# Attention in a conformer block: engine, bank, buffer and order of every key tile from tables

## The chip, the cores and the metric

One core of one Trainium2 chip. A core has five engines that run their own instruction streams and meet through semaphores: TensorE (PE, matrix products into PSUM; PEld is its weight load), ScalarE (ACT), VectorE (DVE), GpSimd (POOL) and SyncE (SP, which here issues most transfers). The metric is the device time of one launch in microseconds; the median of three runs before the change is 894.57 us.

## What is computed

Two sequences of 4000 tokens with 144 features pass through a conformer block: a half-step feed-forward layer, attention with 4 heads of 36 features over all 4000 keys, a gated convolution of 5 taps, a second half-step feed-forward layer, and a layer norm ahead of each and at the end.

```python
B, T, D, K, H = (2, 4000, 144, 5, 4)
h = _layernorm(x)
x = x + 0.5 * (_silu(h @ w_ff1a) @ w_ff1b)
qkv = _layernorm(x) @ w_qkv
scores = jnp.einsum('bhqd,bhkd->bhqk', q, k) * Dh ** (-0.5)
p = _softmax(scores, axis=-1)
x = x + einsum('bhqk,bhkd->bhqd', p, v) (heads joined) @ w_o
a, b = halves of _layernorm(x) @ w_pw1
c = depthwise convolution of a * _sigmoid(b) with dw
x = x + _silu(c) @ w_pw2
x = x + 0.5 * (_silu(_layernorm(x) @ w_ff2a) @ w_ff2b)
return _layernorm(x)
```

## The kernel before

**Tiles.** Tokens are cut into 16 chunks of 500 (8 per sequence). A chunk's queries meet the keys of their sequence in tiles of 64 keys: 62 full tiles and one rest of 32, so 63 per chunk and 1008 in all, numbered `n` in the order of `its`. For a full tile PE makes the scores of four heads with four products of 64x64 (`scores`, two per half `hh`), each filling one quarter of the array, into two PSUM banks of 128 x 500 f32. Six of the eight banks serve scores and all other products; the last two (`BX`, `BX+1`) hold the chunk's output sums.

**Exponentials.** A tile's exponential is made in one of two ways. ACT does it with one activation over both banks (128 x 1000, `emit_exp`), and the result goes to one of 11 buffers `PT`. Or DVE does it (`dve_tile`): one conversion to int16 per half out of PSUM (z), then two bit operations (y and w) and a product (m) between `PT` buffers. The DVE way leaves two factors in two `PT` buffers, and both are multiplied with V. PE then adds a `PT` buffer times V to the output sums (`o_quads`), 4 products for a tile of ACT and 8 for one of DVE. The softmax needs no maximum; a column of ones in V gives the denominator.

**The rest.** `pre` makes the first feed-forward layer and K, Q and V of a chunk; those of the first sequence have to come ahead of its attention, and the ones of the second sequence run between key tiles. So do `post1` (output product, gate) and `post2` (convolution, second feed-forward layer, store) of finished chunks. Sigmoid and SiLU are made with tanh, which lies in one activation table with exp; the last chunks use SiLU itself, for which ACT loads another table. Layer norms take statistics on DVE, the power and the scaling on POOL (`XN`), then a DMA transpose on SP's queue. `ln_trq` copies the transposed chunk into `XTQ` with two DMAs, one for each half of the features.

**Order.** A planner (`Rec.op`, `Sched`, `pick`) simulates the engines with costs (`c_pe`, `c_dve`, `c_act`) and latencies, and so chooses which tile goes to DVE (`due`), which bank and buffer each gets, and the order on each engine. Each step of the planner is a block of instructions. `Rec.reorder` (line 249) then moves the blocks of each engine by up to 45 places with the table `ORDER`, and `PLACES` replaces the planner's choice of banks. `Rec.finish` derives the waits from the dependences, and `Rec.replay` (line 343) emits everything. It emits every instruction at one line, L353, so that the profile's lines say nothing and its groups are told apart by tile names: `PS<-QT,KT` are scores, `PT<-PS` exponentials or DVE's conversions, `PT<-PT` DVE's other operations, `PS<-PT,VA` output sums, `TH<-PS` the tanh.

```python
shift = [ALPHABET.index(c) - 45 for c in table[e]]
...
for i, blk in enumerate(blocks):
    assert at[i + shift[i]] is None
    at[i + shift[i]] = blk
lines[e] = [o for blk in at for o in blk]
```

Of the kernel before, what the change touches and what calls it, by code (L numbers as in the profile page):

```python
# [12 lines left out]
D = 144  # L13
# [20 lines left out]
ALPHABET = '!#$%&()*+,-./0123456789:;<=>?@ABCDEFGHIJKLMNOPQRSTUVWXYZ[]^_`abcdefghijklmnopqrstuvwxyz{|}~'  # L34
ORDER = {
    "pe": (
        'PPPPPPPPPPPPQQRROKPPQRPQLPPQOPPSOROQLQOQOPPPPXPNPUkNOJLPLPQOLPNOOOOPPMOOOOOOOROOPPPQOPPPPPPPTPNPNQTN'
        'PNOROOPQTUMRO]KKOYZZMK]KKKKKOKPHOPRULNPPMPQQNQQNPZOOZOOOOOINNPNPQOPPPPPPPPPPPPPQQQMPQRNQNQOQOQRNQQMQ'
        'SNVVMMWYMMMPNGSMRSSKRSSHRJMQOPPPQOPPPPPPPQOQOQOPPQOPQOPPPQRRMQRLRNOQQQMQOPQQQVLOOOOOPPPQOPPPPPRSNNQN'
        'SSNNQMRPNROOROUNOTNNSMRMRMQNPQQRMOPPQOQQQMPQOPPPQQNPPSPNOPPQOPPQQNPPPPPPPPPPQOQOPQOQOPPQQNPPPPPQOQQQ'  # L40
        'MPQOPPQOPQOPQOPPPQOQQNPPPPQOQOPPPQQQMPPQQQQQKPROQQMPPQOPPQOPQOPQRNQNPPPPPQSNOQNPPPPPPQOPPPPPPQOPPPPP'
        'PPPPPPPPPPPPPPPPPPPPPPRPQQLPPPPSOOOPPPPPPPPPPPPPPPPQOPPPPPPPPPPPPPPPPQRPMQOPQOQQNPQOQQNQOPSOOOPPPPPP'
        'PPPPPPROOQOPPPPPPQOPPQOPPPPPPPPPPPQOPPPPPPPPPPQOQOQRNQNROQNPQQRMQNPPPPPQOPPPPQOPPPPPPPPPPPPPPPPPPPPP'
        'PPPPPPPQOPPSOOOPPQOPPQOQOPPPQRNOQOPQOPQOPPQOPPROQQMQOPQOPPQQNROOPPPPPPPPQOPPQOPPPPQOQOQOPROOPQOPPPQO'
        'SOOOPPQOPPSOOOPPSOOOPPQOPPSOOQNPQOPQOPQSNOQNPSSNRMMRPNPQOPPQQQMPQOPPPQQQQLPROQNPPPPQQNQOQOPPPQQQMQOP'
        'RORNQNPPPPPQSNOQQMQSNOOPPROQQQLPQOPQOPQOPPQOPPPPPPPQOPPPPROOPPSOOOPPQOPPPPPQOPPPPQOPQOQOPPQOSPPQLPQO'
        'QOPPPTOOORNOQQQMPPPPPPPQOPPPPPPQOPPPPQOPPPPPPPPPPPPPPPPPPPPPPQQNPPPPPPPPPPQQQMPRPNQOPPQQQRLOROOQOROO'
        'PPPPPPPPPPPTOSNOMPPPRROMQOVOOOOOOPPPPPPQQNPPPSOOOPPQOPPPPPPPPPPPPPPPPPPPPPQOPPPPPPPPPPQQNQOPQQNQOPPP'
        'QOPPPQOROOPQSNOOPPSOOOPPQOPPPPPPQOPPQOPPPQOROOPSOORNOPPROOPPPQOPPPRPQRROJPPQOQOPPQQNPPPPPQOPPPQOQOPP'
        'PPPPQOPPPPPPQOPPPPPPQOPPPPPPPPPPPPPPPPPPPPPPQOPPPPPPQOPQOPPPPPPPPPPQOPPQOROOQOPPPPPPPQOPPQOPPPQOPPPP'  # L50
        'PPPQOPPPQOPPPROOPPPPPPPPPPPPPPPPPPPPQOQQNPPQOPPQOPQOPPQOPPPPPPPPQOPPPPPPPPPPPROOPPPPPPPROOPPPPPPPPPP'
        'PPPPPPSOOOPPPPPSSNNNPQOPPROOQOPPPPPPPPQOPQQQMPPPPPPPQQNPQOPPTOSNOSLORNOPPQOPPQQNPPTOPRRLRLOPPROOQOTQ'
        'NNOPPPPPPPPPPQOQOPROOPQQNPROOQOPPQOPPQOPPPPPPPPQOPPPPPQOPPQOQOQSNOOPPQQNPQOQOPPPPPPPPPPQOPPQOPPQOPPQ'
        'OTOOOOQQRMQNQOPPPQQNROOPQOPPQRVMNOOROMROOPPPQOPPPPPSOOSNOOPQOPSOOQNPPPPPPPPPPQOPPPPTOOOOPQOPPPPPPPPP'
        'PPPPQOPPPPPPPPPPQOROOPPQOPQOPPROOQOPQQNPQOPQOPPQOPSSNNNQQNPQUNOPNOPPPPQOROOPPQOPPQOPQOPSOOOPPPTOQNNP'
        'PPPQOPPPSOPQMRORRMUPPPPQHPPPPQOQOPPSOOOPUOOOOOPQOPPSOOOPPPPPPPPPPPQRROQRPQQGPTTOMOMROOPPPPPPPPQOROQN'
        'PPQOPPPQOPSOPQMPPRPNPRPNPQOPPPPPPPPPPPPPRPNPQQNPPPPPPPPPPQOPPPROQNPPQQNPPPQOPQOPPPPPPRRNNPPPQOQSNOQN'
        'PTOOOQNPPPPPPPQOPPQQQMPROOPQOPQOQOPPPPQOPPPPPPPPPPPPPPPPPPPPPQOPPPPPPPPPPPPPPPPPPPPROOPPQOQOPQOROOSO'
        'OUNOOUNPQLQMPROOPQOPROOQQQQQKPQOPPPPPPQOPPPQOPQRNRNQNQQQMRRSNLQNQOPQOPPPPPPPROOPPPPPPPPPPPQOPPPQOPQO'
        'PROOPQQNPPQQNPPPPPPPPPQOPQOPPROOROOPPQQTMOPNPPPPPPRPNPPQOPPPPPPPPPPPPPRPQSPKOQQQMPPPRORNQNPROOPRRNNR'  # L60
        'OQNPQOQQNPPPPPPROOPPQOPPQOPPPROQRMRRMNQOPQOPQQNPROOQOPPPPPPPPQOPPPPPPPPRPNPPSOOQNQOPSOOOPPPPPPPPPPPP'
        'PPPPPPPPQOQOPQRNQNPPPPPPQOPPPPPPPPPPPPPQORRNNPPPPPPPPPPPPQOPPQOPPPQQQQLPQOQOPPPPPPPPPUOQNSOLOPQOQOPP'
        'QQQMPRPNPPPPPPPQQNPPROOPQOPQOQQNPPPQOQOPPQOSOOTNOOOWQTMMNNNPQOPPPPPSOOQNSPNQSMRNRMQQMPPTOPVMPTLPRLRP'
        'JPPQOPPRPNQQNPPPPPPQOPQOPPQOPQOPPPPPROOQSNOOPROQNPPPPPQQQMPPQOPPQOPPPPPPQOPPQORRRRLLPPPQRNOPRd`R[^MO'
        'SOYQYLLQNUUVWU:Q9;=BPQXPXRKRLLLMOPPPPPPQOPPQRNQUQRPRUVQOWOROQUSZTR;=JKOQNQMPPQQQMSPNO'
    ),
    "act": (
        'PPPPPPPPPPQQRMOPPQOPPPPPPPPPPPPPQQRPLQOQOPPPPPQOPPPPPPPPPPPPPPPPPPQOQOPPPQOPPQOQOPPPPQOPQOPPPPPPPPPP'
        'PPPPPPPPPPPPPPPPPPPPPPPPPPPPPPPPPPPPPPPPPPPPPPPPPPPPPPQOPPPPPPPPPPPPPPPPPPPPPPPPPPPPPPPPPPPPPPPPPPPP'
        'PPPPPPPPPPPPPPPPPPPPPPPPPPPPPPPPPPPPPPPPPPPPPPPPPPPPPPPPPPPPPPPPPPPPPPPPPPQOPPPPPPPPPPPPPPPPPPPPPPPP'  # L70
        'PPPPPPPPPPPPPPPPPPPPPPPPPPPPPPPPPPPPPPPPPPPPPPPPPPPPPPPPPPPPPPPPPPPPQOPPPPPPPPPPPPPPPPPPPPPPPPQOPPPP'
        'PPPPPPPPPPPPPPPPPPPPPPPPQOPPPPPPPPPPPPPPPPPPPPPPPPPPPPPPPPPPPPPPPPPPPPPPPPPPQOPPPPPPPPPPPPPPPPPPPPPP'
        'PPPPPPPPPPPPPPPPPPPPPPPPPPPPPPPPPPPPPPPPPPPPPPPPPPPPPPPPPPPPPPPPPPPPPPPPPPPPPPPPPPPPPPPPPPPPPPSOOOPP'
        'PPPPPPPPPPPPPPPPPPPPPPPPPPPPPPPPPPPPQOPPPPPPPPPPQOPPPPPPPPPPPPPPPPPPPPPPPPPPPPPPPPPPPPPPPPPPPPPPPPPP'
        'PPPPPPPPPPPPQOQOPPPPPPPPPPPPPPPPPPQOPPPPPPPPPPPPPPPPPPPPPPPPPPQOQOPPPPPPQOPPPPPPPPPPPPPPPQOPPPPPPPPP'
        'PPPPPPPPPPPPPPPPPQOPPPPPPPPPPPPPPPPPPPPPPPPPPPPPPPPPPPPPPPPPPPPPPPPPPPPPPPPPPPPPPPPPPPPQOPPPPPPPPPPP'
        'PPPPPPPPPPPPPPPPPPPPPPPPPPPPPPPPPPPPPPPPPPPPPPPPPPPPPPPQOPPPPPPPPPPPPPPPPPPPPPPPPPPPPPPPPPPPPPPPPPPP'
        'PPPPPPPPPPPPPPPPPPPPPPPPPQOPPRPNPQQRSQNJQQNPPPPPPPPPQQQQQQVPPPQSSCLWMOOOPNO'
    ),
    "dve": (  # L80
        'PPPPPQQNPPPQQQMPPQOROOPPROOPTOQUMQLPXLOOOOOTOMOOPPPPQOQQNQOPPQORPTPLPNPPPQOPPPQWNQNNOOOPPPPRSNPMPQRN'
        'QNROOQOPPPPPQOPQOPPPRPQRLOPPPPPPPPPPPQOQQNPPPPQQRPQQJQQQQQRPQQQQQQQRPQSPPQQQRRRR5RRRRSLROTRORRM>PPQT'
        'PMPNQQNPPQOPPROOPPPPPQQQMQQNPQOPQOPPQOPPPPPPPPPPPPSOOOPQOPPPPPPPPPPPPPPPPPPQOPPPPQOQQNPPPPPPPPQOPPPQ'
        'OPPQQRPQQRIQRPLPPPPPPPPPPPPPPPPPPPPPPPPPPPQRNOQQNQOPPPPQOPQOPPPPPPPPPPPPPROOPRPNPPQOPPPPPPPPPPPPPPPP'
        'PQOPPPPPPPPQOQRPMPROOPPPQOPPPPPPPPQOPPPPPPPPPPQOQOPPPQOPQOPPPQOPQOPPPPPPPPPPPPPPPVPQOPPQQQGPPPPPPQOP'
        'PPPPPPPPPPPQOSPNOPPPPPPPPQOPPPPPPPPQOPPPPPPPPPPPQRPMPPPPPPPQOPQOPQOPPPPPQOQOPPQOQOQOPPQOPPQOPPPPPPPP'
        'PPTOPPQLQQNROQQMPPPQOPPPPPPPROOPPPQOQOPPPPPPPPPPPPPPPPPPPPPPPPPPPPPPPPPPPQOPPPPPPPPPPPPPPPPPPPPPPQOP'
        'PPPPPPPPPPPRRNQMPPPPQOQOQQNPPPPPPPPROOROOPPPPPPPPPPPPPPPPPPPPPPPPPPPPPPPPPQOQOPQOPPPPPPPPQQNPPPPPPPP'
        'PPROOPPPPPPPPRPNPQOQOPPPPQOPPPPPPRPNPPPPPPROOPPPQOQOPPPWOOOOQOMQOPPPROOPROOPPQOPPPPPQOPPSOPNPPPPPPPP'
        'PPPQOPPQOQOPPROOQOPPQOPPPQOPPQQNPPPQOPPQOQOQRPQLQOPPPPPPPQOPPPPPPPPPPPQOPPPPPPPPPPPPPPPPPPPPPQOPPPPP'  # L90
        'PPQOQOPPPPPPPPPPPPPPPQRNOROSNRNNPPPPPPeOOOPNOOOOOPNOOOPNOOOPPQOQOPPPPPQOPPQOPPPPPPaOSNRMNLOOPNPPMOOP'
        'ROQNQQQMPQOPPPPPPPPPPPPPPPPPQOPPPPPPXOOOOPNOOPPPPPPQUPMOOQNQOPPQOP]PNOOOOPNQNNOPPQQNPPPQOPPPQOPPPROO'
        'PPPQOQOPQOPPPPPROOQOPPRORNOPPPPPPPP^OOOVOMNPMOLOOPQQNPPPPPPPPPPPPPROOPPPPPPPPPPQOQOPRPNPPPPP_OOOOOOO'
        'OPNOPPRPKQOPQOQOPPQOPPPPPPPPQQNPPPPPRPNPROQNPPQOPQOPPPPPQOPPPPPPPPPPPQOPPPPPPPPPPPPPROOPPPPQOPPPPPPP'
        'PPROOPPQOPPPQOPPPPPQOPPPPQOQOQOPPPPPPPPPPPPPPPPPPQQQRPKPQOPPPPPQOPQOPPPQOROOPVPNOOOOPQOPPPPPPPPPPPPP'
        'PPPPPPQOPPROOPPPPPPPPPPPPPPQOPQOPRSNSTLMP^LSNOMNPNPQOROSXPGMRNSSMKRSQNIPPUOUOMNNOPPPPPQRPQLQOQOQORRU'
        'NL[PQMKOQNPQLSPPTZUYGX`WIZHHJKKFOINNPQLPPPSOOO'
    ),
    "pool": (
        'PPPPPPPQOPSUNQNRRRRRSTRVVVPUUUUVVVIUU6TV>RRS3RRRS;PRPQQ=QOSOOOPQOTPPPLPR]OMORPMMOaNNNROLNOOZNOMOMSPM'  # L100
        'OJROOPQOPUOPNOOXOOPNOOOOPPSOPQMQRPM'
    ),
    "sp": (
        'PPPPPPPPPPPPPPQOQOPPPPPROOQOPPQORORNOQTNOOTNOOOPQOPPQTNOOSNOOTOOPQMPPSOOQQMPPUOOOOOTOOOOQOPPQO'
    ),
# [31 lines left out]
def c_act(n):  # L137
    return n / 1200 + 0.051
# [10 lines left out]
class Rec:  # L149
# [22 lines left out]
    def op(self, eng, name, *a, r=(), w=(), q=None, cost=0.1, kind=None, lat=None, **k):  # L172
# [1796 lines left out]
```

## Time and profile before

| what | us |
|---|---|
| median of 3 runs | 894.57 (894.15 to 894.78) |
| the profiled execution's own time | 893.85 |
| its span, first to last instruction | 892.0 |
| first exponential, last exponential (starts) | 19.9, 837.2 |
| first, last conversion on DVE (starts) | 82.8, 833.7 |
| POOL waiting for statistics of DVE | 467.9 in all, 39 waits |

The span is what the instructions cover; 1.85 us lie around it in the same execution. The granted clock of TensorE is 1.0 throughout. How far the engines are filled over time is in the page's 40 slices (each digit a tenth, 9 is 90% or more):

```
PE   8999999999999999999999999999999999999997
DVE  8877888999999999999999998889998999998996
ACT  6999999999999999999999999999999999999763
POOL 6744041350143107103212142252125141503433
```

PE's row is busy time of pipelined products whose ends are modelled, so a full row isn't a PE at its peak. The chain of work that ended last is put down to ACT for 59% of the span, to PE for 33% and to DVE for 6%.

### The profile page before, as it was taken

What the parts mean: (1) busy time and instruction counts of PE and PEld (TensorE: products, weight loads), DVE (VectorE), ACT (ScalarE), POOL (GpSimd) and SP (SyncE); (2) the same over time, 40 slices, a digit from 0 to 9 for tenths busy, and PEclk for the clock granted to TensorE, in tenths of its full rate; (3) what the DMA queues carried; (4) which work ended last, traced back from release to release, by engine and by line L of the source; (5) the groups of instructions that cost most, each with busy time, mean ns of one, the idle gap of its engine ahead of it and who ended that gap; (6) DMA issues with size and microseconds to landing.
All of it is one profiled execution on the core that took longest, in us unless ns stands there. A gap on an engine that the chain in (4) does not pass through costs nothing.

```text
span 892.0 us, 27205 instructions
## 1 busy us (share of the span) xinstructions
PE 863.8 (97%) x11731; PEld 395.8 (44%) x11731; DVE 815.7 (91%) x1786; ACT 847.6 (95%) x1084; POOL 277.6 (31%) x543
## 2 busy tenths in 40 slices
PE   8999999999999999999999999999999999999997
PEld 7444334344443434334343444343434344444587
DVE  8877888999999999999999998889998999998996
ACT  6999999999999999999999999999999999999763
POOL 6744041350143107103212142252125141503433
PEclk9999999999999999999999999999999999999999
DMA  4413011210212011401120010102010210111001
GB/s 122 66 31 53 5 37 32 43 26 14 32 39 44 7 25 21 67 1 26 31 26 2 13 33 14 31 13 39 13 25 14 38 25 13 33 20 25 20 15 34
DMA packets 83422, 26.13 MB, mean 29 GB/s; under 512 B 78226, under 2 KB 83302, under 8 KB 83302
## 3 DMA queue, kind: packets, MB, share of 16 engines
q1 hardware_dynamic: 81624, 23.56, 14.5%
q8 instruction: 92, 1.51, 0.7%
q10 hardware_dynamic: 1678, 0.84, 0.4%
q14 instruction: 28, 0.23, 0.1%
HBM read 3.31 MB, written 2.30 MB: 6 GB/s over the span
## 4 chain that ended last, share of the span: by engine, by line
ACT 59%; PE 33%; DVE 6%; DMA 1%; issue 0%; POOL 0%; SPq 0%; POOLq 0%; DVEq 0%
ACT PT L353 53%; PE PS L353 33%; ACT TH L353 5%; DVE PT L353 4%; DMA XTB<-XN 1%; DMA X<-in_x_dram 0%; DVE ST L353 0%; DVE HT L353 0%; DVE X L353 0%; DVE KT L353 0%; DVE XN L353 0%; POOL RS L353 0%; ACT L353 0%; DVE QT L353 0%; DVE AN L353 0%
## 5 line engine op out<-in xcount | busy, mean ns | idle before, releaser
L353 ACT ACTIVATE PT<-PS 128x1000 bf16<-128x1000 f32 x815 | 753.0, 1066 | 2.9 <-PE PS L353 1.3
L353 PE MATMUL PS<-QT,KT 64*64 64x500 bf16 x3968 | 423.1, 384 | 13.6 <-ACT PT L353 6.8
L353 PE MATMUL PS<-PT,VA 64*37 64x500 bf16 x4740 | 417.7, 373 | 2.2 <-DVE QT L353 1.0
L353 DVE TENSOR_SCALAR PT<-PS 128x500 int16<-128x500 f32 x386 | 255.3, 670 | 19.8 <-PE PS L353 17.4
L353 PEld LDWEIGHTS PS<-QT,KT 64*64 64x64 bf16 x3968 | 125.0, 104 | 237.8 <-ACT PT L353 143.7
L353 PEld LDWEIGHTS PS<-PT,VA 64*37 64x37 bf16 x4740 | 140.5, 96 | 101.7 <-DVE PT L353 20.1
L353 POOL TENSOR_SCALAR RS<-ST 125x4 f32<-125x4 f32 x118 | 30.8, 261 | 473.7 <-DVE ST L353 467.9
L353 DVE TENSOR_SCALAR PT<-PT 128x1000 uint16<-128x1000 uint16 x386 | 154.1, 414 | 1.6
L353 POOL TENSOR_SCALAR XN<-X,RS 125x144 bf16<-125x144 bf16 x236 | 129.3, 562 | 6.2
L353 DVE TENSOR_TENSOR PT<-PT 128x1000 bf16<-128x1000 bf16 x193 | 129.7, 676 | 1.5
L353 ACT ACTIVATE TH<-PS 128x500 bf16<-128x500 f32 (+3 forms) x189 | 104.0, 565 | 8.1 <-PE PS L353 7.1
L353 POOL TENSOR_TENSOR RS<-RS,NHALF 125x4 f32<-125x4 f32 (+2 forms) x97 | 92.1, 952 | 53.0 <-DVE RS L353 48.1
L353 DVE SCALAR_TENSOR_TENSOR HT<-TH,PS 128x500 bf16<-128x500 bf16 (+1 forms) x130 | 79.1, 614 | 10.2 <-ACT TH L353 9.3
L353 PE MATMUL PS<-XTB,WA 72*128 72x500 bf16 (+2 forms) x296 | 73.2, 350 | 2.3 <-DMA XTB<-XN 1.0
L353 DVE SCALAR_TENSOR_TENSOR X<-PS,X 125x288 bf16<-125x288 f32 (+1 forms) x128 | 57.2, 451 | 14.3 <-PE PS L353 13.3
L353 DVE BATCH_NORM_STATS2 ST<-X 125x6 f32<-125x288 bf16 x160 | 66.1, 448 | 1.1 <-DMA X<-in_x_dram 0.7
L353 PE MATMUL PS<-WB,HT 128*125 128x144 bf16 (+1 forms) x640 | 52.4, 229 | 0.3 <-DVE U L353 0.2
L353 PEld LDWEIGHTS PS<-WB,HT 128*125 128x125 bf16 (+1 forms) x640 | 44.7, 136 | 13.3 <-issue 5.6
L353 POOL COPY U<-U 128x2 bf16<-128x2 bf16 (+1 forms) x54 | 12.3, 269 | 76.7 <-DVE U L353 62.1
L353 PEld LDWEIGHTS PS<-XTB,WA 72*128 72x128 bf16 x296 | 21.2, 97 | 32.1 <-issue 10.9
L353 PE MATMUL PS<-U,DG 128*128 128x250 bf16 (+6 forms) x204 | 29.8, 264 | 0.1
L353 PE MATMUL PS<-IDENT 128*128 128x128 bf16 x341 | 24.2, 226 | 1.5 <-POOL NHALF L353 1.5
(89 smaller groups left out, 537.0 us busy)
## 6 DMA issues: line engine op xcount, KB each, us to landing
X<-in_x_dram SPq DMA_DIRECT2D x16, 140.6 KB
XTQ<-XTB SPq DMA_DIRECT2D x24, 70.3 KB
out_dram<-XN SPq DMA_DIRECT2D x11, 140.6 KB
XTB<-XN SPq DMA_TRANSPOSE x50, 3.2
out_dram<-XN SPq DMA_DIRECT2D x4, 70.3 KB
XTB<-AN SPq DMA_TRANSPOSE x15, 3.3
out_dram<-XN ACTq DMA_DIRECT2D x3, 70.3 KB
WA<-in_w_ff1a_dram ACTq DMA_DIRECT2D x1, 144.0 KB
```

Of the source, the lines that this page charges most:

```text
L353: ins = getattr(eng, o.name)(*o.a, **o.k)
```

## The change

Four new tables replace the planner's choices for the key tiles. `TYPES` has one letter for each tile: A (ACT), D (DVE, half by half), W (DVE, both halves in one conversion of 1000 columns), R (the rest tile, ACT). `BANKS` has two score banks for each tile, `SLOTS` two `PT` buffers. `ORDER` no longer has shifts but the place of every block, in two characters, on each engine, and the blocks of the key tiles are finer: each half's scores, and each (factor, half p) of the output sums, is a block of its own. The planner still runs, with new costs, latencies and policy tables, and its blocks outside attention are kept; then `settle` throws its key tile instructions away, makes them anew from the tables, and `arrange` puts everything into the tables' order and derives the dependences on banks and `PT` buffers from that order. The first sum of each (phase, p, hh) in PE's order gets `start`, the last gets `stop`.

```diff
-ALPHABET = '!#$%&()*+,-./0123456789:;<=>?@ABC...
 ORDER = {
     "pe": (
...
+        '!!!#!$!%!&!(!)!*!+!,!-!.!/!0!1!3!5!2!6!4!7!9!8!;!<)^)_!:!=)b)c)g)f!>)j)k!?!@)n)o!A!B)r)s)w)v!C!E!J!F'
...
+TYPES = (
+    'AAAAAAAAAAAAAAAAAAAADAAAAADAAAAADAAAAAADAAAADAAAAADAAAADAAAADDAAAADAAAADAAAAADAAAAAAAAAAAAAADAAAAAA'
...
+BANKS = (
+    '4512451245124545014501452345232301230134454523234501450145014501234501450145013245014501304501451234'
...
+SLOTS = (
+    '%!!!)!&!$!,!(!#!%!&!#!%!,!+!(!&!-!$!!!+!*(#!-!)!,!$!(!-!+!&!%!-!,!+!)!$!+!*!)!%!&!#!-!+!$))!*!(!#!&!'
...
-    LAT = dict(pe=0.165, act=0.12, dve=0.083, pool=0.1, sp=2.0)
-    SEM = dict(pe=0.053, dve=0.036, act=0.045, pool=0.08, sp=0.1)
-    SWITCH = 0.095
+    LAT = dict(pe=0.185, act=0.2, dve=0.09, pool=0.25, sp=2.0)
+    SEM = dict(pe=0.053, dve=0.037, act=0.036, pool=0.08, sp=0.03)
+    ISSUE = 0.0035
+    SWITCH = 0.1
...
-    def reorder(self, table):
+    def arrange(self, table, readers, slots, users):
...
+            keys = sorted(blocks, key=lambda q: (isinstance(q, tuple), q))
+            at = [ALPHABET.index(x) * 90 + ALPHABET.index(y) for x, y in zip(table[e][::2], table[e][1::2])]
+            assert sorted(at) == list(range(len(keys)))
+            lines[e] = [o for i in at for o in blocks[keys[i]]]
...
         for o in lines["pe"]:
             k = o.tile
+            if k is not None and k not in seen:
+                seen.add(k)
+                for b in self.places(k):
+                    if b in last:
+                        o.deps += [(d, False) for d in readers[last[b]]]
...
+            if o.att is not None and o.att[1] == "O":
+                n, _, j, p, hh = o.att
+                if (n, j) not in used:
+                    used.add((n, j))
+                    writers, sums = users[n, j]
+                    prior = held.get(slots[n, j])
+                    if prior is not None:
+                        for w in writers:
+                            w.deps += [(d, False) for d in users[prior][1]]
+                    held[slots[n, j]] = (n, j)
...
-    NXN, NXT, NTH, NHT, NSW = 5, 5, 4, 3, 3
+    NXN, NXT, NTH, NHT, NSW = 5, 5, 6, 3, 3
...
-    NAN = 5
+    NAN = 4
...
-                   w=[("XTQ", c % CPB, i) for i in bs] + [("LANE", j)], cost=0.6, lat=LAT_C)
+                   w=[("XTQ" if k == 0 else "XTR", c % CPB, i) for i in bs] + [("LANE", j)], cost=0.8, lat=LAT_C)
...
+    def ff_wide(s, h, m, WA, nm):
+        bks, t = yield need("pe", (wide, thw), dur=0.84)
...
+        op("act", "activation", TH[:, t:t + 2, :], ps, ACT.Tanh, bias=0.0, scale=0.5, r=rk, w=[("TH", t)],
+           cost=c_act(2 * CH))
...
+    def table():
+        if mode["front"]:
+            return ["TAB0"]
+        if not mode.get("table"):
+            mode["table"] = True
+            R.step += 1
+            op("act", "activation", DUM[:, :], NHALF[:, 0:1], ACT.Silu, bias=0.0, scale=1.0, r=["NHALF"],
+               w=["DUM", "TAB0", "TAB1"], cost=1.4)
+            R.step += 1
+        return ["TAB1"]
...
+    def settle():
...
+        for n in range(NIT):
+            ph, c, t = its[n]
+            rest = t == NF
+            kind = TYPES[n]
+            assert (kind == "R") == rest
+            bk = [int(v) for v in BANKS[2 * n:2 * n + 2]]
+            sl = [ALPHABET.index(v) for v in SLOTS[2 * n:2 * n + 2]]
...
+                if kind == "D":
+                    zs = []
+                    for hh in range(2):
+                        a, k = z_args(sl[0], hh, bk[hh])
+                        zs.append(fresh("dve", "tensor_scalar", a, k, COST["z"], "e", [(o, True) for o in S[hh]],
+                                        (n, f"z{hh}"), hh))
+                        readers[n, hh, bk[hh]] = [zs[-1]]
+                else:
+                    assert bk[1] == bk[0] + 1
+                    a, k = z_args(sl[0], 0, bk[0], bk[1])
+                    zs = [fresh("dve", "tensor_scalar", a, k, COST["x"], "e", both, (n, "z"), 5)]
...
+                        k = dict(k, start=False, stop=False, skip_group_check=True)
+                        o = fresh("pe", "matmul", a, k, COST["S"], "w" if rest else "q",
+                                  [(d, True) for d in ready] + v_deps + list(sum_deps.get(ph, {}).values()),
+                                  (n, "O", j, p, hh), 2 + 2 * j + p, (2 * p, 2 * p + 1) if rest else (2 * p + hh,),
+                                  0.2 if rest else None)
...
-    if ORDER is not None:
-        R.reorder(ORDER)
+    if TYPES is not None:
+        settle()
```

The new order table has 5020 blocks on PE, 1071 on ACT (805 of them exponentials), 1688 on DVE, 139 on POOL and 97 on SP; the old one has 1075 on ACT (815 exponentials) and 1646 on DVE (193 tiles of 5 blocks). `table()` puts one tiny SiLU activation ahead of the first SiLU of the last chunks, as a block of its own. The XTQ line lets the second DMA of a pair go without waiting for the first. `ff_wide` makes two tanh of a feed-forward layer in one instruction where the policy `FFW` is 1, in one of 49 stretches.

## The prediction

> **What bounds the kernel now.** I read the page's first part, then the windows, the forms, the chain of waits, and the waits themselves.
>
> ```profile
> PE 863.8 (97%) x11731; PEld 395.8 (44%) x11731; DVE 815.7 (91%) x1786; ACT 847.6 (95%) x1084; POOL 277.6 (31%) x543
> ```
>
> Three engines are over 90%, so the share alone decides nothing. The windows cut the span (892.0 us) at the first exponential (19.85) and behind the last (841):
>
> ```profile
> core 0: us, PE busy (x) PEld busy (x) DVE busy (x) ACT busy (x) POOL busy (x), PEclk, DMA share, GB/s
> 50.00:100.00 50.00, 49.11 (x620) 21.31 (x616) 37.90 (x82) 47.55 (x63) 15.25 (x31) 1.00 0.22 40
> 19.85:841.00 821.15, 801.21 (x10857) 338.52 (x10856) 758.11 (x1584) 812.82 (x1009) 247.48 (x487) 1.00 0.15 28
> 841.00:892.00 51.00, 45.61 (x639) 42.24 (x636) 41.44 (x145) 23.74 (x53) 16.84 (x26) 1.00 0.07 22
> ```
>
> For 821 us ACT idles 8.3 us; behind that, a 51 us tail without exponentials has ACT half idle. The forms say what ACT and DVE do:
>
> ```profile
> L353 ACT ACTIVATE PT<-PS 128x1000 bf16<-128x1000 f32 x799 | 745.7, 1074 | 2.9 <-PE PS L353 1.3
> L353 DVE TENSOR_SCALAR PT<-PS 128x500 int16<-128x500 f32 x386 | 255.3, 670 | 19.8 <-PE PS L353 17.4
> L353 DVE TENSOR_SCALAR PT<-PT 128x1000 uint16<-128x1000 uint16 x386 | 154.1, 414 | 1.6
> L353 DVE TENSOR_TENSOR PT<-PT 128x1000 bf16<-128x1000 bf16 x193 | 129.7, 676 | 1.5
> ```
>
> So 799 full key tiles are ACT's and 193 are DVE's. The mean of 1074 ns overlaps the next instruction; the pace is in the chain (start, length, what):
>
> ```profile
> 249.57 32.90 ACT PT L353 x37
> ...
> 542.30 18.08 ACT PT L353 x20
> ...
> 850.53 1.28 ACT L353
> 851.82 0.60 ACT SW L353
> ...
> 852.47 32.85 PE PS L353 x444
> ```
>
> 32.90/37 is 0.889 us each; 18.08/20 is 0.904, so some exponentials are held up inside what counts as busy. ACT's account for the 821 us: 799 x 0.889 = 710.3; 157 activations of 500 columns at the 0.48 us between chain starts = 75.4; 25 of 250 at 0.27 = 6.8; 28 narrower at 0.16 = 4.5; together 797. **ACT is the bound, and loses 24 us of 821**: 8.3 idle, 16 hidden in late exponentials. DVE idles 63 us.
>
> ```profile
> PEld PS L353 <- ACT PT L353: 152.2, 402, 0.8
> ```
>
> PE's weight loads wait 152 us for ACT to empty score banks: PE is mostly the one kept waiting.
>
> **The change, part by part.** *Types.* The type table has 789 A, 201 D, 2 W and 16 R. Against 799, 193 and 16 ACT loses ten full exponentials: 10 x 0.889 = **-8.9 us** on the bound engine. DVE takes them. A D tile is two conversions, two bit operations and a product: back to back 2 x 0.59 + 2 x 0.33 + 0.59 = 2.43 us (starts in DVE's timeline), by the busy sums above 2 x 0.661 + 2 x 0.399 + 0.672 = 2.79; a W tile has one conversion of 1000 columns (the f32 copy of that size starts its follower 1.11 us later), much the same. Ten cost 24 to 28 us. They lie in DVE's 63 us of idle time; uncovered, they would be the whole cost. The first D moves to tile 20; today DVE's first conversion starts at 82.8 us, after 42 exponentials, and 50 to 100 has 12.1 us of DVE idle. PE gets 4 more sums per tile, at 0.0525 each (four run side by side in 0.21): 2.1 us, covered by its waits.
>
> *Orders.* Every sum (one half p of one tile) and score half becomes its own block and may stand anywhere. PE pays when it turns between attention products and others:
>
> ```profile
> 305.69 0.38 PE L353 MATMUL PS<-PT,VA 64*37 64x500 bf16 x4
> 305.90 0.37 PE L353 MATMUL PS<-QT,KT 64*64 64x500 bf16 x2
> ...
> 310.12 0.38 PE L353 MATMUL PS<-PT,VA 64*37 64x500 bf16 x4
> 310.43 0.28 PE L353 MATMUL PS<-WP,SW 128*125 128x144 bf16 x1
> ```
>
> A foursome followed by attention takes 0.21 us, followed by another product 0.31: 0.10 lost. Counted along PE's rows there are 720 such turns; the new PE table has 656. 64 x 0.10 = 6.4 us less of PE, when scores are what ACT waits for.
>
> What of ACT's 24 us goes? The tables put sums where their inputs are ready, and rows show both ends: nothing (the lost time is latency of score, exponential, bank, and stays), or nearly all (0.889 was held for 33 us), say 18; if static orders meet other durations, it grows. I take **-8 us**, a third, near the 6.4 of the turns.
>
> *Tail.* In the chain a table load of 1.28 us stands at 850.53 before the SW activation. The new `table()` makes it an instruction that the order may put into ACT's idle time: 0 to -1.3. Orders of the last 51 us: 0 to -2, or some us worse, since ACT has 70 blocks behind its last exponential (59 instructions now). I take **-1**.
>
> *Small ones.* The two DMAs that fill XTQ get separate keys:
>
> ```profile
> SPq L353 <- DMA XTQ<-XTB: 21.3, 12, 2.6
> ```
>
> Twelve waits of 1.8 us on SP go; queued behind them are transposes and stores of other chunks, and SP waits 286 us for POOL anyway: 0; were a chunk's projection the last to arrive, -1.8 each. One AN buffer less, two TH buffers more, one wide feed-forward pair (at most one 0.05 us of fixed cost): 0. Six fewer other DVE blocks and six more on ACT (one the table load) are copies of 0.48 us that the planner gives ACT only in front and tail, where it idles: 0, at worst 2.4. Waiting on every earlier sum of a bank adds no instruction: 0 if the counter has passed; else one late sum holds all PE work queued behind it, ACT's next scores first, which the growing end above holds.
>
> *Against it:* DVE's tile work stretches POOL.
>
> ```profile
> L353 POOL TENSOR_SCALAR XN<-X,RS x31: 462/465/469, 21.5 to 81.6; 125x144 bf16<-125x144 bf16 x31
> L353 POOL TENSOR_SCALAR XN<-X,RS x204: 457/464/1389, 114.1 to 834.2; 125x144 bf16<-125x144 bf16 x102
> ```
>
> Before DVE's first tile no normalisation exceeds 469 ns; later some take 1389. With D tiles from tile 20 this comes into the front: some 20 normalisations there, 0.92 us more for the worst, the mean of all 236 (562 ns on the page of forms, against 465) 0.1 us more: 2 us, spread over POOL's 35 us of idle time in 50 to 100: 0, at worst +3. "SBUF — State Buffer" of the Trainium skill, section Who interferes with whom, says that VectorE and GpSimd shut each other out of a shared port for a whole instruction. By that rule ten more tiles could close POOL's port for 10 x (2 x 0.33 + 0.59) = 12.5 us, an estimate from the rows above; the rows show the stretch, but only in a few instructions, so the sum keeps the 0.
>
> **Sum:** 892.0 - 8.9 - 8 - 1 = 874.1 us of span. The profiled run took 893.85 (1.85 around its span), the median 0.72 more: 876.7.
>
> **Rivals.** *Only the ten:* the lost 24 us are latencies that no order removes: 883.1, time 885.7. For it: PE, ACT and DVE hand each tile on, and an order was already tabled. Against: the pace of 0.889 holds over 37 in a row.
>
> *Nearly all comes back:* -8.9, -18, -3: 862.1, time 864.7. Against it: 656 turns remain.
>
> *PE sets the end:* its 97% says so, and the chain has PE for 33%. Then 2.1 us of sums are added and the turns give 0 to 6.4 back: time 890.3 to 896.7, middle 893.5. "Perfetto Trace Analysis", section Identifying the Most-Contended Engine, in the Trainium skill, calls matmul busy time a poor measure because matmuls are pipelined. Against this rival is the 152 us that weight loads wait for ACT.
>
> *DVE becomes the bound (slower):* in the stretch it then has 758 + 28 - 3.5 (six blocks at 0.59) = 783 us of work. If its 63 us of idle are waits for scores (17.4 are named so) that stay, the stretch is 846, 25 longer; it decides once over 821 - 783 = 38 us of them stay. The mechanism: a D tile's conversion late on DVE keeps its score bank, PE cannot write the next scores, ACT starves. Halfway, 50 staying: 12 longer, 904, time 906.6. For it: DVE would be 97% busy in 804 us. Against: from 400 to 500 DVE is already 96.1 of 100 busy with ACT at 99.7; 4% of 821 is 33, under 38.
>
> **How the numbers follow.** Forecast 0.55 (own range 868 to 884); only the ten 0.14; nearly all 0.12; PE 0.05; DVE 0.14. About 0.2% (1.8 us) can be told from no change. Faster: 0.55 + 0.14 + 0.12 and 0.01 of PE's, 0.82; same 0.04; slower 0.14. The range, 864 to 892, takes in the first three and half of PE's case, and leaves out the slower one and some of the low end.
>
> **What would show it.** 789 full exponentials at 0.89 us a piece in the long chain pieces; ACT's lost time in the exponential stretch near 16 us instead of 24; that stretch near 804 us; DVE near 97% there; fewer waits of DVE for scores than 17 us; the first DVE conversion before 60 us; no table load in the last chain; no SP wait between the XTQ pair. The forecast is wrong if the exponentials are slower than 0.90 on average, if DVE waits push bank releases behind ACT's pace, or if the tail is longer than 52 us.

## The result, and the profile after

The changed kernel takes **888.36 us** (median of 4 runs, 887.88 to 888.64) against 894.36 for the kernel before beside it: a ratio of 0.9932 [0.9915, 0.9950]. The forecast was 876.7. The profiled execution takes 888.42 with a span of 886.6; the prediction's sum was 874.1, so the span missed by 12.5 us. The page's first part:

```profile
PE 868.6 (98%) x11752; PEld 419.7 (47%) x11752; DVE 832.4 (94%) x1824; ACT 838.5 (95%) x1074; POOL 279.0 (31%) x544
```

DVE has 16.7 us more work and ACT 9.1 less. The windows, cut at 100 us, at the first exponential and where the last one's follower starts:

```profile
50.00:100.00 50.00, 48.99 (x701) 20.68 (x693) 44.25 (x91) 48.44 (x59) 15.24 (x30) 1.00 0.17 23
19.99:828.66 808.67, 798.80 (x10854) 357.81 (x10853) 774.32 (x1619) 795.30 (x982) 244.34 (x480) 1.00 0.16 28
828.66:886.60 57.94, 52.67 (x702) 46.94 (x699) 43.40 (x147) 32.37 (x71) 21.09 (x35) 0.99 0.10 25
```

Before, the same cuts lie at 19.85 and 837.68:

```profile
19.85:837.68 817.83, 797.89 (x10836) 336.40 (x10834) 755.64 (x1580) 809.76 (x1003) 247.48 (x487) 1.00 0.15 28
837.68:892.00 54.32, 48.93 (x666) 44.36 (x658) 43.91 (x148) 26.80 (x60) 16.84 (x26) 1.00 0.07 20
```

The stretch with exponentials is 9.2 us shorter and the tail 3.6 longer; with 0.14 for the later start that is the whole 5.4. What ACT and DVE do, in the page's forms:

```profile
L546 ACT ACTIVATE PT<-PS 128x1000 bf16<-128x1000 f32 x789 | 734.9, 1090 | 6.5 <-PE PS L546 5.0
L546 DVE TENSOR_SCALAR PT<-PS 128x500 int16<-128x500 f32 x402 | 263.9, 672 | 13.0 <-PE PS L546 10.4
L546 DVE TENSOR_TENSOR PT<-PT 128x1000 bf16<-128x1000 bf16 x203 | 137.0, 678 | 1.5
```

Ten exponentials have gone, as counted from the table. **ACT's account of the stretch**, with the prediction's own prices and the counts that the forms have inside each stretch, so that both kernels are read alike: before 799 x 0.889 + 152 x 0.48 + 24 x 0.27 + 28 x 0.16 = 794.2 of 817.8, 23.6 lost; after 789 x 0.889 + 142 x 0.48 + 24 x 0.27 + 26 x 0.16 = 780.2 of 808.7, **28.5 lost**. The prediction had 16. So the stretch became shorter by 14.0 us of work (8.9 of exponentials, 4.8 of 500-column activations that now come behind the last exponential, 0.3 of narrow ones) and longer by 4.9 of lost time. Where that loss is, two windows show, before and after, in which only ACT's column (the fourth busy time) is to be read:

```profile
20.00:50.00 30.00, 28.62 (x335) 14.20 (x333) 25.71 (x66) 28.39 (x44) 22.03 (x41) 1.00 0.35 59
200.00:400.00 200.00, 196.10 (x2728) 81.45 (x2730) 191.88 (x396) 199.01 (x241) 48.72 (x94) 1.00 0.17 28
```

```profile
20.00:50.00 30.00, 28.31 (x327) 16.98 (x329) 29.53 (x74) 23.63 (x42) 16.12 (x30) 1.00 0.40 62
200.00:400.00 200.00, 198.57 (x2762) 87.29 (x2762) 192.02 (x401) 198.61 (x241) 52.69 (x108) 1.00 0.16 31
```

From 20 to 50 us ACT is busy 4.8 us less; from 200 on it runs as full as before. The forms from 200 to 800 us say the same in tiles, before

```profile
L353 ACT ACTIVATE PT<-PS 128x1000 bf16<-128x1000 f32 x603 | 563.4, 1078 | 2.0 <-PE PS L353 0.7
L353 DVE TENSOR_TENSOR PT<-PT 128x1000 bf16<-128x1000 bf16 x161 | 108.2, 675 | 1.2
```

and after:

```profile
L546 ACT ACTIVATE PT<-PS 128x1000 bf16<-128x1000 f32 x604 | 562.2, 1093 | 2.8 <-PE PS L546 1.7
L546 DVE TENSOR_TENSOR PT<-PT 128x1000 bf16<-128x1000 bf16 x163 | 109.6, 676 | 1.2
```

764 tiles in 600 us before, 767 after. The middle of the kernel gained almost nothing; the lead was made ahead of 200 us, where DVE finishes 31 products instead of 22. The same form in the first 200 us, before and after:

```profile
L353 DVE TENSOR_TENSOR PT<-PT 128x1000 bf16<-128x1000 bf16 x22 | 14.9, 679 | 0.2
```

```profile
L546 DVE TENSOR_TENSOR PT<-PT 128x1000 bf16<-128x1000 bf16 x31 | 21.1, 683 | 0.3
```

The chain of waits (start, length, what) shows what the front and the tail hang on now:

```profile
27.38 21.41 PE PS L546 x232
...
95.00 18.05 ACT PT L546 x20
...
821.09 58.73 PE PS L546 x763
```

The piece from 27.38 to 48.8 is PE's: feed-forward products of later chunks run there (28 tanh before 50 us instead of 20), and only 10 exponentials instead of 18. The waits that the prediction named:

```profile
PEld PS L546 <- ACT PT L546: 145.7, 426, 0.7
DVE PT L546 <- PE PS L546: 11.8, 36, 1.0
```

Both fell a little. In the tail the last chain is PE for 58.73 us without a break. A part of it, from PE's timeline (start, length, what) and then from DVE's:

```profile
858.13 0.79 PE L546 MATMUL PS<-WB,HT 128*126 128x144 bf16 x10
858.76 5.52 PE L546 MATMUL PS<-IDENT 128*128 128x128 bf16 x96
864.12 0.39 PE L546 MATMUL PS<-IDENT,XN 125*72 125x125 bf16 x4
```

```profile
861.10 0.54 DVE L546 TENSOR_SCALAR XN<-X,ST,RS 125x144 bf16<-125x144 bf16 x2
```

The 96 products of the identity with itself are fillers: they compute nothing and keep PE running while it waits. What PE waits for, the norm XN, ends at 861.64; PE transposes it at 864.12, when the fillers are through. Counting busy time hides this: PE is "busy" for 2.5 us that nobody needs.

### The profile page after: what moved, and what is told of

It is laid out like the page before. It is cut to its first block, busy times and chain, and to the rows that moved or that the text cites. A ratio compares the mean times of both kernels' runs of the same rounds, so it can differ in the third digit from the quotient of the medians.

```text
span 886.6 us, 27318 instructions
## 1 busy us (share of the span) xinstructions
PE 868.6 (98%) x11752; PEld 419.7 (47%) x11752; DVE 832.4 (94%) x1824; ACT 838.5 (95%) x1074; POOL 279.0 (31%) x544
## 3 DMA queue, kind: packets, MB, share of 16 engines
q8 instruction: 92, 1.51, 0.7%
## 4 chain that ended last, share of the span: by engine, by line
ACT 53%; PE 41%; DVE 4%; DMA 0%; issue 0%; POOL 0%; POOLq 0%; DVEq 0%
ACT PT L546 49%; PE PS L546 41%; ACT TH L546 4%; DVE PT L546 1%; DVE XN L546 1%; DVE ST L546 1%; DMA X<-in_x_dram 0%; DVE HT L546 0%; POOL RS L546 0%; DVE XTB L546 0%; DVE X L546 0%; DVE QT L546 0%; DVE KT L546 0%; DVE VA L546 0%; POOLq L2349 0%
## 5 line engine op out<-in xcount | busy, mean ns | idle before, releaser
L546 ACT ACTIVATE PT<-PS 128x1000 bf16<-128x1000 f32 (+1 forms) x805 | 742.3, 1082 | 6.5 <-PE PS L546 5.0
L546 PE MATMUL PS<-QT,KT 64*64 64x500 bf16 x3968 | 458.0, 384 | 7.1 <-ACT PT L546 2.1
L546 PE MATMUL PS<-PT,VA 64*37 64x500 bf16 x4780 | 447.4, 373 | 1.4 <-DVE QT L546 0.5
L546 DVE TENSOR_SCALAR PT<-PS 128x500 int16<-128x500 f32 x404 | 266.3, 675 | 13.1 <-PE PS L546 10.4
L546 PEld LDWEIGHTS PS<-QT,KT 64*64 64x64 bf16 x3968 | 137.5, 104 | 218.6 <-ACT PT L546 133.4
L546 PEld LDWEIGHTS PS<-PT,VA 64*37 64x37 bf16 x4780 | 160.4, 96 | 108.0 <-issue 20.2
L546 POOL TENSOR_TENSOR RS<-RS,NHALF 125x4 f32<-125x4 f32 (+1 forms) x99 | 93.7, 949 | 55.6 <-DVE RS L546 50.3
L546 DVE BATCH_NORM_STATS2 ST<-X 125x6 f32<-125x288 bf16 (+1 forms) x160 | 66.4, 448 | 3.1 <-DMA X<-in_x_dram 2.5
L546 PE MATMUL PS<-U,DG 128*128 128x375 bf16 (+5 forms) x204 | 28.1, 263 | 0.0
L546 ACT ACTIVATE HT<-PS 128x500 bf16<-128x500 f32 (+3 forms) x46 | 21.8, 526 | 6.1 <-PE PS L546 5.8
```

The lines of the kernel that those rows point to most:

```text
L546: ins = getattr(eng, o.name)(*o.a, **o.k)
```

## The experiments

All times are medians beside runs of the kernel before on the same chip (893.7 to 894.4); "lost" is ACT's stretch less its work, taken from each trace with the shortest pace of each kind of activation (0.884 for a full exponential), by which before has 29.9 and after 34.6: a difference of 4.7, where the account above has 4.9.

**Are the exponentials on ACT what counts?** Nine D tiles go back to ACT, as two 500-column activations each, once in the front (tiles 20 to 61), once in the middle (400 to 446):

```diff
+            elif kind == "H":
+                es = []
+                for hh in range(2):
+                    es.append(fresh("act", "activation", (PT[:, sl[0], hh, :], PSV[:, bk[hh], 0:CH], ACT.Exp),
...
-    'AAAAAAAAAAAAAAAAAAAADAAAAADAAAAADAAAAAADAAAADAAAAADAAAADAAAADDAAAADAAA...
+    'AAAAAAAAAAAAAAAAAAAAHAAAAAHAAAAAHAAAAAAHAAAAHAAAAAHAAAAHAAAAHHAAAADAAA...
```

> The changed kernel (888.4) with the first nine D tiles (20 to 61) given back to ACT, as two activations of 500 columns each into the same banks and buffer; their DVE operations and second sums go, all other orders stay. Theory A (the change gains by exponentials taken off ACT, and only so): 9 x 2 x 0.47 = 8.5 us more on the bound engine, about 897, slower than before the change. Rival B (at the front ACT waits for scores anyway: it lost 8.4 us before 50 us and 3.0 in the kernel before): the nine are hidden in those waits, at most +3, about 890.

> The same with nine D tiles between 400 and 446, in the middle of the stretch. Theory A: again +8.5, about 897. Rival C (by now DVE and PE bound the middle as much as ACT: DVE is 94% busy, PE 98%): what ACT takes on is given back by DVE's 9 x 2.43 = 22 us and PE's 2 us of relief, and the time rises by under 4 us, about 891.

Measured: 896.27 (1.0023 [1.0009, 1.0036]) and 896.78 (1.0035 [1.0015, 1.0055]), spans 7.8 and 8.3 above the changed kernel's. Lost: 34.0 and 35.0. Each tile is worth 0.87 to 0.92 us, about what its exponential takes on ACT (0.88 in one piece, 0.93 in two halves), in the front and in the middle alike, and taking nine tiles' work from DVE and 36 sums from PE gave ACT nothing back. Theory A held, B and C fell.

**What is the order of the sums worth?** The two p halves of each factor's sums stand side by side, at the place of the earlier one; only PE's row of `ORDER` differs, as in its first line:

```diff
-        '!G!I!H!D!P!K!S!L!M!N!Q!R)i)h)a)t)e)`)q)p)y)l)d)m!T!O!W!U!V!]!a!Y!X!^!`!_!c!Z![!b!e!h!g!i!d!f!k!j)z){'
+        '!G!I!H!D!P!K!S!L!M!N!Q!R)i)h)a)`)t)u)e)d)q)p)y)x)l)m!T!O!W!U!V!]!a!Y!X!^!`!_!c!Z![!b!e!h!g!i!d!f!k!j'
```

> The free order of the sums undone: the two halves p of each factor's sums stand together, at the place of the earlier one; all else stays. Theory A: order brings nothing, the scores' latency decides: 888.4 within 1.5. Rival D (the free order is worth what my forecast took, some 8 us, and hides a loss elsewhere): 893 or more.

Measured: 901.54 (1.0083 [1.0061, 1.0106]), span 899.1, lost 47.6. The waits:

```profile
DVE PT L546 <- PE PS L546: 22.4, 66, 1.1
ACT PT L546 <- PE PS L546: 8.1, 22, 1.0
```

DVE waits for scores almost twice as long as in the changed kernel (11.8), and ACT's waits grow from 5.0; the loss comes in many steps of 0.2 to 0.5 us all along the stretch. Theory A fell: within the new tables the free order of the sums carries 12.5 us. That doesn't say that it gained as much over the old order; it says the tables are laid out around it.

**Is ACT's lost time PE's work?** The second factor's sums run over 4 columns instead of 500 (that part of the sums is left out), in the changed kernel (the diff) and, by the same cut in `o_quads`, in the one before.

```diff
+            if o.att is not None and o.att[1] == "O" and o.att[2] == 1 and all(o is not q for q in first.values()):
+                o.a, o.k["rhs"] = (o.a[0][:, 0:4],), o.k["rhs"][:, 0:4]
```

> The output sums of the second factor of each DVE tile run over 4 columns instead of 500 (but for a group's first sum): this part of the sums is left out, and PE has some 200 x 0.0525 x 4 x (a fourth of what a tile of four sums takes) to 200 x 0.21 us, so 10 to 40 us, less work in the stretch; order, waits and ACT's work are those of the changed kernel. Theory H (the 34.6 us that ACT loses are PE's turn-taking: scores stand behind sums): ACT's lost time falls by 6 us or more, 882 or less. Rival I (they are latency from score to exponential to bank, or the planned order itself): within 1.5 us of 888.4, lost time 33 to 36.

> The kernel before with the output sums of the second factor of each DVE tile run over 4 columns instead of 500: this part of the sums is left out, and PE has some 35 us less work in the exponential stretch (in the changed kernel the same cut took the sums' busy time from 448 to 417 us), several times the 6.4 us that the prediction hoped for from fewer turns; order and waits stay. Theory Q (PE's work, turns included, was among what ACT lost time to, as the prediction's step has it): ACT's stretch 6 us shorter or more, 888.5 or less. Rival R (ACT's lost time is latency and order in the kernel before too): within 1.5 us of 894.4.

Measured: 891.52 (0.9967 [0.9956, 0.9978]) for the first, 892.04 (0.9981 [0.9973, 0.9990]) for the second. The kernel before has then 13 us less on PE and is 0.9 us shorter in span, 1.7 by the ratio:

```profile
PE 850.5 (95%) x11731; PEld 390.7 (44%) x11731; DVE 816.3 (92%) x1786; ACT 846.5 (95%) x1084; POOL 278.5 (31%) x543
```

Its lost time goes from 29.9 to 29.2, so R held in what it says of the lost time, with a trace of Q: its number, within 1.5 us, was just missed, and Q's 6 us are far off. The changed kernel with less PE work is 0.8 us ahead at 580 us (0.2 of it from its start), and then loses 4.6 in one place. PE's timeline (the idle time ahead in brackets), and windows with the granted clock behind the five busy times:

```profile
578.25 0.60 PE L549 MATMUL PS<-XTB,WP 72*128 72x500 bf16 x2
580.76 0.60 PE L549 MATMUL PS<-XTB,WA 72*128 72x500 bf16 x2 [1.90 <-DMA XTB<-XN]
```

```profile
580.00:582.00 2.00, 1.24 (x18) 0.53 (x22) 0.29 (x2) 0.59 (x1) 0.00 (x0) 1.00 0.00 0
582.00:584.00 2.00, 2.00 (x19) 0.48 (x12) 1.97 (x5) 1.19 (x2) 0.00 (x0) 0.54 0.00 0
584.00:586.00 2.00, 2.00 (x12) 0.59 (x14) 0.95 (x2) 1.40 (x3) 0.00 (x0) 0.50 0.00 0
```

PE arrives early, idles 1.9 us for a transpose, and then its clock is about half for some 7 us, in which scores come late and ACT is busy 1.2 to 1.6 of each 2 us. Elsewhere the lost time is the changed kernel's within 0.5, as theory I says; its number (within 1.5 us of 888.4) was missed through this one stall. Of the six timed runs, the one whose mean clock is a full 1.000 took 888.72 us, the others, at 0.994 to 0.998, 889.91 to 892.30. So even without the loss of clock the cut brought nothing, and H fell.

**Can DVE take still more?** Nine and three further full tiles become W tiles on DVE, with a second `PT` buffer that is free then, by edits of `TYPES`, `SLOTS` and `ORDER`; one line of the types of the kernel with three:

```diff
-    'DAAADAAADAAADAAADAAAAAAAADAAADAAAADAAAADAAADAAAAAAARDAAAADAAAAADAAADAAADAAAAADAADAAAAADAADAAADAAAAD'
+    'DAAADAAADAAADAAADAAAAAAAADAAADAAAADAAAADAAADAAAWAAARDAAAADAAAAADAAADAAADAAAAADAADAAAAADAADAAADAAAAD'
```

> Nine more full key tiles, spread from 110 to 800 us of the changed kernel's trace, go from ACT to DVE as W tiles (one conversion of 1000 columns, two bit operations, one product), with a second PT buffer that is free at that time; all else of the changed kernel stays. Theory A (ACT's work is what the stretch pays for, as the runs that gave tiles back to ACT say): 9 x 0.884 = 8.0 us less, about 880.4, ACT's stretch near 800.7 us with the lost time unchanged at 33 to 36 us. Rival G (DVE, busy 94%, is full: nine tiles of 2.4 us are 21 us more, late conversions hold score banks): 888 or more, ACT's lost time up by 8 or more, and DVE above 96% in the stretch.

> Three full key tiles (at 240, 547 and 782 us of the changed kernel's trace) go from ACT to DVE as W tiles; nine of them took 27.5 us more. Theory S (each tile too many costs its stall at its own place, 27.5 / 9 = 3.1 us): +9, about 897.6, ACT's lost time near 46 us. Rival T (DVE has room for a few, and only nine overfilled it): -2.6, about 885.8, lost time at 35. A number between 888 and 894 would say that room is there at some of the places.

Measured: 915.94 (1.0254 [1.0225, 1.0282]), lost 70.4; and 898.65 (1.0050 [1.0038, 1.0061]), lost 47.9, of which +6 come within 17 us behind the tile at 240. DVE's, PE's and ACT's timelines of the kernel with three:

```profile
240.28 1.19 DVE L546 TENSOR_SCALAR PT<-PS 128x1000 int16<-128x1000 f32 x1
...
242.88 0.67 DVE L546 CAST KT<-PS 128x500 bf16<-128x500 f32 x1
```

```profile
243.61 0.77 PE L546 MATMUL PS<-XTQ,WK 72*128 72x500 bf16 x2 [1.69 <-DVE KT L546]
```

```profile
244.99 1.00 ACT L546 ACTIVATE PT<-PS 128x1000 bf16<-128x1000 f32 x1 [2.02 <-PE PS L546]
```

The inserted conversion makes the copy of KT late, the copy frees a bank, PE stands 1.69 us before the next projection with the scores queued behind it, and ACT starves for 2.02; behind it the granted clock is 0.50 from 244 to 250. G and S held (G's DVE share of over 96% did not come: 794.81 us of the stretch's 836.54, 95%, since DVE waits too). The places weren't searched again, so this shows that the placed tables have no slack there, not that DVE could take none in any order.

**Tail.** All 203 fillers are left out (`no_fill`); the run of 96 is cut to 54 and the run of 24 taken out (`trim_fill`); the other runs of 4 and more as well (`trim_more`); and in the kernel before the run of 69 is cut to 30 (`before_trim`):

```diff
+    for o in [o for o in R.ops if o.eng == "pe"] + [None]:
+        if o is not None and id(o) in late_ids:
+            run.append(o)
+            continue
+        for low, keep in ((90, 54), (24, 0)):
+            if len(run) >= low:
+                gone.update(id(q) for q in run[keep:])
```

> The 128-column filler products with the identity that the planner put into the tail's waits of PE are left out there (203 of them behind the last exponential, 11.4 us of PE). Theory E (the tail grew by 3.6 us because the planner's fillers no longer fit the order: 96 of them hold PE from 858.8 to 864.1 though the normalised tokens that the next transposes read are there at 862.5, and 24 from 869.8 to 871.1 though theirs are there at 869.6): 3 to 4 us less, about 885. Rival F (the tail is 3.6 us longer because it holds more work, eight tanh and their products moved behind the last exponential): fillers stand in idle time, 888.4 within 1; or, if they keep PE's clock up, slower.

> In the tail the run of 96 filler products (IDENT x IDENT) is cut to 54 and the run of 24 is taken out; the other fillers stay. The fillers compute nothing that is used. Theory J (these two runs are longer than the waits they fill, and the products behind them start late): 2 to 4 us less, about 885.4, the tail behind the last exponential near 55 us. Rival K (what comes behind waits for data anyway): within 0.7 us of 888.4. Rival L (the gaps left lower the granted clock, as with no fillers at all): 888.4 to 890, granted clock below 0.9 in a stretch of the tail.

> trim_fill with all other filler runs of 4 and more in the tail taken out as well (16 cut to 6). Theory J, carried on (fillers that stand ahead of ready products cost their own time, 0.056 us each where PE is in the chain): 1 to 2 us less than trim_fill, about 884. Rival L (too much idle time lowers the granted clock): above 886, granted clock below 0.9 in a stretch of the tail.

> The kernel before with its one long run of filler products in the tail (69 ahead of 852.47) cut to 30. The fillers compute nothing that is used. Theory Z (before, the run filled a real wait, for ACT's table load and the norm that ends at 852.4; too many fillers are the new order's own fault): within 0.7 us of 894. Rival (the old tail has the same excess): 1.5 to 2.2 us less.

Measured: 889.21 (0.9965 [0.9940, 0.9989]); **885.25 (0.9906 [0.9893, 0.9919])**; 886.22 (0.9918 [0.9897, 0.9939]); 896.32 (1.0022 [1.0007, 1.0038]). With the two runs trimmed PE goes straight from its fillers into the transposes, 3.1 us earlier (0.7 of it was there already ahead of the fillers, where the two kernels do not differ), and the tail is 55.4 us instead of 57.9:

```profile
858.03 3.18 PE L546 MATMUL PS<-IDENT 128*128 128x128 bf16 x54
861.04 0.39 PE L546 MATMUL PS<-IDENT,XN 125*72 125x125 bf16 x4
```

So J held: of the 3.1 us between the medians, the tail accounts for 2.5. Without any fillers, E's 3 to 4 us less did not come either; 889.21 lies within 1 us of the changed kernel, as rival F has it. In that run's trace (898.13 us, late already from the front, where its clock stood at 0.50 from 30 to 40 us) the windows of the tail read:

```profile
865.00:870.00 5.00, 1.68 (x24) 1.53 (x25) 4.59 (x19) 1.39 (x4) 2.56 (x4) 1.00 0.27 78
870.00:875.00 5.00, 5.00 (x37) 3.65 (x35) 1.29 (x6) 2.72 (x6) 0.76 (x2) 0.66 0.13 39
```

PE idles 3.3 us, and the products behind run at a clock of 0.66. The fillers aren't waste; only their number is off. `trim_more` gained nothing on `trim_fill` (its six runs reach from 885.25 to 892.38), so theory J, carried on, fell, and what rival L says came: its clock is at 0.50 from 870.1 to 876.9, where `trim_fill` has 1.00 until its last instructions. The old tail gained nothing by trimming either: it takes 54.3 us in both traces, so its long run did cover a real wait, for a norm and ACT's table load. The median rose by 2 us, more than Z allowed. The traced execution (895.04) does not show where; the trimmed run leaves PE idle (0.33 of 2 us busy from 852 to 854), and most of the slower executions have a mean clock of 0.992 to 0.997, so a loss of clock is likely, but not shown.

**Work in the tail.** In the late feed-forward layers 4 of 5 slices are made over 60 columns instead of 500; the rest of these hidden values is left out.

```diff
+            w = 60 if m < 4 else n
+            op("act", "activation", dst[:, 0:w], PSV[:, bk, 0:w], ACT.Silu, bias=0.0, scale=1.0,
```

> In the feed-forward layers made with SiLU in the tail, the 4 full slices of hidden values of each late chunk get 60 columns of products and activation instead of 500; the rest of these values is left out. PE loses about 1.5 us per chunk of two, ACT as much. Theory M (the tail is longer because more work was moved behind the last exponential, and its amount sets the end): 2 to 3 us less, about 886. Rival N (the tail is the last chunk's own chain of norm, transpose, product and store, with its waits; amounts are hidden): within 0.7 us of 888.4.

Measured: 887.48 (0.9939 [0.9919, 0.9959]), tail 57.3 us. The tail is 0.6 us shorter for 3.0 us less busy time of these products on PE (4.4 to 1.4) and as much less of these activations on ACT (14.6 to 11.6): N held. The activations that moved behind the last exponential are by this run probably nearly free there.

**The front.** PE's accumulating products of instructions 202 to 560 run over 8 columns; the rest of these sums is left out.

```diff
+        for o in lines["pe"][202:560]:
+            if o.kind == "f" and o.name == "matmul" and not o.k["start"]:
...
+                    out, rhs = out[:, 0:8], rhs[:, 0:8]
```

> Of PE's instructions 202 to 560 (about 20 to 52 us) the accumulating products of the layers ahead of attention run over 8 columns instead of 72 to 500; the rest of these sums is left out. That takes some 8 us of PE's column work out of the front. Theory U (PE sets the front, where the chain of waits has it from 27.4 to 48.8 us, and ACT loses 8.4 us there): ACT's lost time before 50 us falls by 3 us or more, and the whole kernel ends 3 to 6 us earlier, 882.5 to 885.5. Rival V (norms on DVE and POOL and the transposes set the front): within 1 us of 888.4.

Measured: 896.91 (1.0032 [1.0020, 1.0044]). Neither: the granted clock, by slices of 22 us on the page, fell in the front,

```profile
PEclk9569999999999999999999999999999999999999
```

and ACT fell 10 us behind by 65 us. All five timed runs lie above 894.8, so it was no single accident, though the traces of `no_fill` and of the kernel with nine more tiles show that the clock can fall there in the unchanged front too (for 20.5 and 6.8 us; here for 41). The run says nothing on who sets the front, since it slowed the engine that it was to relieve.

**The XTQ wait.** Put back into the changed kernel, and taken out of the kernel before, as the only edit:

```diff
+    for a, b in pairs:
+        b.deps.append((a, False))
```

> The wait of the second DMA that fills XTQ for the first is put back, all else is the changed kernel. The prediction's price of 0: within 0.7 us of 888.4, with some 12 waits of 1.8 us on SP in the queue's waits again. Rival W (transposes or loads queued behind them come late): 1.5 us more or worse.

> The kernel before with one step of the change alone: the second DMA that fills XTQ no longer waits for the first. Theory X (only the new order, which places the projections close behind their data, lives on the earlier arrival; the old one was laid out with the wait): within 0.7 us of 894. Rival Y (the wait costs the old order as well, as putting it back costs the new one 8 us): 3 us less or more, 891 or below.

Measured: **896.89 (1.0048 [1.0028, 1.0068])**, lost 42.2, and 894.09 (1.0000 [0.9991, 1.0010]). The waits with it put back:

```profile
SPq L546 <- DMA XTQ<-XTB: 23.9, 13, 3.2
PE PS L546 <- DMA XTQ<-XTB: 6.3, 6, 1.9
```

The changed kernel has neither line. The new order puts the projections so close behind their data that PE now stands at six of them; at 434.9 us for 1.93 us, after which the clock reads 0.54 and 0.61 in the 2 us windows from 438 to 442 and the exponentials are 3.3 us later. W and X held: worth nothing in the old order, 7.1 us of span in the new one.

## Why the prediction was off

- **"Ten exponentials x 0.889 = -8.9"** held. The count is 789, the pace is the same, and nine tiles given back cost 7.8 and 8.3. Their cover held too: 24 to 28 us of DVE work were priced at nothing, DVE took 16.7 us more in all, and ACT gained what it gave.
- **"I take -8 us, a third" of the lost time** is the step that failed. It came out as +4.9, 12.9 us off; the sum missed by 12.5. In the prediction's own split, the 16 us hidden in late exponentials, which the orders were to give back in part, stayed (15.5 before and 15.1 after, by the account above), and ACT's idle time grew from 8.1 to 13.4. The reason given for it, 64 fewer turns of 0.10 us on PE, did come about: counted along PE's instructions in both traces, the turns went from 720 to 656. But it named a resource that ACT wasn't waiting for: 13 us of PE's busy time taken from the kernel before shortened its span by 0.9 us, 1.7 by the ratio. From 200 to 800 us the lost time is 18.6 before and 17.9 after: a whole new order of PE, ACT and DVE gave 0.7 there. What would bring the rest back stays open: the runs show what adds to it, and none that takes from it. The rows quoted "from both ends" (0.889 held over 37, 0.904 over 20) said how much was lost, and nothing on what would bring it back. The prediction had the rival for this, "only the ten" at 883.1 us of span, and gave it 0.14; the span is 3.5 above that: 4.9 of lost time, 3.6 of tail and 0.1 of later start, less 5.1 of activations that left the stretch.
- **The front** was only priced as a stretch of POOL (0, at worst +3). The exponentials per time were not: the new order runs feed-forward products first, ACT idles 4.8 us more from 20 to 50 us, and DVE's tiles from 58.75 us on (forecast: before 60) make up for it. Whether another front order would have kept both stays open.
- **"Tail -1"** came out as +3.6, with 4.8 us of activations moved into it that the stretch no longer has; together -1.2. That this lies near the forecast is luck: neither the moved activations nor the fillers were in it. The prediction's own sign, a tail over 52 us, came (54.6 by its cut, 3.3 us behind the one used here). The table load was indeed taken off the chain: it runs right behind the last exponential, as ACT's timeline has it,

```profile
828.66 0.88 ACT L546 ACTIVATE TH<-PS 128x500 bf16<-128x500 f32 x2
829.56 1.28 ACT L546 ACT_TABLE_LOAD   x1
```

  and what it freed, and more, went into fillers: 2.5 us of tail come back by trimming two runs, which the prediction didn't look at.
- **"XTQ: 0"** was right for the old order, and the price of the wait "were a chunk's projection the last to arrive" was what applied in the new one, some six times. An edit's worth was read off the kernel before, though the tables were laid out for the kernel with the edit.
- **POOL's stretch: 0** held. The normalisations mean 567 ns on the page against 562 before, 1.2 us over 236. "SBUF — State Buffer" of the Trainium skill, section Who interferes with whom, would by the prediction's estimate have closed POOL's port for 12.5 us more; this trace doesn't show it, though the longest single one now takes 1685 ns (1389 before).
- Of the rivals, **PE** as the bound (now 98% and 41% of the chain) fell by the runs with less PE work. **DVE as the bound** didn't come about with these ten tiles (95.7% busy in the stretch; forecast 97), but the mechanism, a late DVE block that keeps a bank from PE until ACT starves, is what the runs with three and nine more tiles show.

## What to carry to other kernels

An engine's lost time isn't a reserve because it is there: ask which resource it waits for, take a large piece of that resource's work away in thought (or in a run), and only count on what then returns. Price an edit in the order it will run in: a wait that costs nothing in the old order can carry the new one, and parts of a searched plan aren't additive (undone one at a time, the nine front tiles, the free sums and the XTQ keys cost 7.8, 12.5 and 7.1 us, of a change that gave 5.4). Where an engine is kept busy by fillers, look at when their input is ready, not at the busy share: the version with two runs trimmed is the best here, 885.25.

## What the hardware did that was not expected

A short stall of PE costs more than itself. 1.90 us idle for a DMA (at 578.9), 1.69 for a copy (at 241.9) and 1.93 for a DMA (at 434.9) were each followed by a granted clock of 0.50, for 6.8, 6.8 and 3.4 us, beginning 1.4, 0.3 and 1.4 us after PE went on. With columns taken out of products in the front the clock was at half for 41 us. "TensorE: Matmul & The Clock Gate" of the Trainium skill, section Part 1: The HAM clock gate, puts the fall behind an idle window of about 3.4 us.

The traces bear out the length: in each of the 17, all changes of the clock lie whole multiples of 3.41 us apart (2, 2, 1 and 12 of them in the four cases above). They don't bear out that the window must be idle. Cut at these points, the first case reads (PE's busy time first, the clock behind the five busy times):

```profile
578.73:582.14 3.41, 1.51 (x19) 0.58 (x22) 1.70 (x4) 1.81 (x3) 0.00 (x0) 1.00 0.00 0
582.14:588.97 6.83, 6.83 (x50) 2.07 (x43) 4.54 (x9) 4.66 (x6) 0.00 (x0) 0.50 0.00 0
```

PE was busy for 1.51 us of the window ahead of the fall, for 1.56 and 1.48 in the other two stalls, and for 2.47 in the front. Over all 17 traces, from 12 us on, no fall came behind a window with more than 2.47 us, and every window with less than 1.48 was followed by one; between the two, some were and some weren't. So it looks like little work in a window, not a whole idle one, that brings the fall. By this reading, where the windows happen to begin decides whether a given stall costs anything more, which would explain why executions of one kernel differ as those with cut sums do; the runs don't show that. A sharper limit can't be read from these runs, the less as the ends of PE's products are modelled.
